# Attention by token chunks over all heads, with TensorE's order written out by hand, half chunks paired across batches, and float32 loads cast on the chip

## The chip, the cores and the metric

The kernel runs on one core of a Trainium2 chip. The metric is the device time of one execution in microseconds (us). A core has TensorE (PE in the profile, with its weight loads as PEld), VectorE (DVE), ScalarE (ACT), GpSimd (POOL), a sync engine (SP) and 16 DMA engines.

## The reference

Eight batches, eight heads, 576 tokens, head width 64: a retention attention, and on its output a mixer with a low-rank token part and an MLP of width 2048. All inputs and the output are float32.

```python
# q, k, v: (8, 8, 576, 64)
scores = q @ k.T / sqrt(64)
gamma  = 1 - 2.0 ** (-5 - arange(8))                 # one per head
Dmat   = where(i >= j, gamma ** (i - j), 0)
x      = ((scores * Dmat) @ v)                       # heads joined: (8, 576, 512)
h      = x.transpose(0, 2, 1) @ U @ V                # U (576, 32), V (32, 576)
u      = x + h.transpose(0, 2, 1)
out    = u + relu(u @ w_ch1) @ w_ch2                 # (512, 2048), (2048, 512)
```

The decay splits into a factor of the query's position and one of the key's, so that a chunk of tokens needs its own masked scores and one 64 by 64 state per head (the sum of k transposed times v over the chunks before it).

## The kernel before

576 tokens are four chunks of 128 and one of 64 (`NC` = 5). All matmuls are in bfloat16.

`qkv_load(b)` loads a batch on POOL's DMA queue, one load for each of q, k, v and each chunk (L141); the load casts float32 to bfloat16 on its way. It clears the half chunk's other 64 rows (L138), and POOL multiplies v by `vscale`, the key factor (L150).

`attention_hp` treats one pair of heads over all five chunks. It transposes q (L164) and k (L174); the copies out of PSUM are DVE's with the query factor `qsrow` (L167) and ACT's (L177). The state products of four chunks (L185) are summed by DVE in pieces of 64 rows (L195, L200). Scores are matmuls of 64 rows, eight into `blk_sc` (L219) and two for the last chunk, `blk_sct` (L238), masked by DVE (L227, L244). Then come the matmuls with v (L256), the copy to `x_t` (L264, L265), the matmuls of 64 rows with the state (L271), and DVE adds these to `x_t` (L280, L286). PSUM pool `ps_sc` has two buffers, `ps_out` one tile of two banks.

`mixer_head(b)` forms `ps_at` from U and x (L301), copies it (L308), makes `ps_h` for each chunk with V (L312), adds x (L318), transposes u (L325) and copies to `uT_t` (L330).

`mlp_tail(b)` computes W1 in 16 blocks of the width and two halves of 288 tokens, four matmuls each (L341) with the Relu behind (L347), then W2 for each of five chunks, 16 matmuls of 512 columns (L356); the fifth has 64 rows, which takes as many columns. DVE adds u (L363), SP stores (L367).

The main program loads batches 0 and 1 and the weights, does the attention of batch 0, and then for each b: loads b+2, `mixer_head(b)` at high priority, `attention(b+1)`, `mlp_tail(b)`. A planner sets the order of every engine's instructions: it takes what its own timing has ready, earlier program text first, and puts in the semaphores. So attention matmuls fill in among MLP matmuls.

Of the kernel before, what the change touches and what calls it, by code (L numbers as in the profile page):

```python
# [12 lines left out]
ALU = mybir.AluOpType  # L13


@with_exitstack
def kernel(
# [18 lines left out]
    NC = (S + P - 1) // P  # L36
    LAST = S - (NC - 1) * P
    SP = NC * P
# [3 lines left out]
    MAIN = (NC - 1) * P  # L42
    HTOK = 288

    gammas = [1.0 - 2.0 ** (-5.0 - h) for h in range(H)]
    scale = 1.0 / math.sqrt(D)

    consts = ctx.enter_context(tc.tile_pool(name="consts", bufs=1))
    qkv_pool = ctx.enter_context(tc.tile_pool(name="qkv_pool", bufs=3))
    attT_pool = ctx.enter_context(tc.tile_pool(name="attT_pool", bufs=2))  # L50
    ret_pool = ctx.enter_context(tc.tile_pool(name="ret_pool", bufs=4))
    ssb_pool = ctx.enter_context(tc.tile_pool(name="ssb_pool", bufs=8))
    xu_pool = ctx.enter_context(tc.tile_pool(name="xu_pool", bufs=2))
    mix_pool = ctx.enter_context(tc.tile_pool(name="mix_pool", bufs=2))
    y1_pool = ctx.enter_context(tc.tile_pool(name="y1_pool", bufs=2))
    osb_pool = ctx.enter_context(tc.tile_pool(name="osb_pool", bufs=4))

    ps_sc = ctx.enter_context(tc.tile_pool(name="ps_sc", bufs=2, space=bass.MemoryType.PSUM))
    ps_out = ctx.enter_context(tc.tile_pool(name="ps_out", bufs=1, space=bass.MemoryType.PSUM))
    ps_mix = ctx.enter_context(tc.tile_pool(name="ps_mix", bufs=1, space=bass.MemoryType.PSUM))  # L60
    ps_big = ctx.enter_context(tc.tile_pool(name="ps_big", bufs=3, space=bass.MemoryType.PSUM))

    ident = consts.tile([P, P], BF16)
    make_identity(nc, ident)

    maskbin = consts.tile([P, P], BF16)
    make_upper_triangular(nc, maskbin, val=1.0, diag=True)

    iota_col = consts.tile([P, SP], FP32)
    iota_pc = consts.tile([P, NC], FP32)  # L70
    lnbias = consts.tile([P, 1], FP32)
    qsrow = consts.tile([P, NHP, SP], BF16)
    vscale = consts.tile([P, H, NC], FP32)
    U_sb = consts.tile([P, NC, P], BF16)
    V_sb = consts.tile([P, SP], BF16)

    def make_early_consts():
        nc.gpsimd.iota(
            iota_pc, pattern=[[P, NC]], base=0, channel_multiplier=1,
            allow_small_or_imprecise_dtypes=True,  # L80
        )
        nc.gpsimd.memset(lnbias, math.log(scale))
        for h in range(H):
            g = gammas[h]
            nc.scalar.activation(
                out=vscale[:, h, :],
                in_=iota_pc,
                func=AF.Exp,
                bias=lnbias,
                scale=-math.log(g),  # L90
            )

    def make_consts():
        nc.gpsimd.iota(
            iota_col, pattern=[[1, SP]], base=0, channel_multiplier=0,
            allow_small_or_imprecise_dtypes=True,
        )

        for hp in range(NHP):
            for hl in range(2):  # L100
                g = gammas[2 * hp + hl]
                nc.scalar.activation(
                    out=qsrow[hl * 64:(hl + 1) * 64, hp, :],
                    in_=iota_col[hl * 64:(hl + 1) * 64, :],
                    func=AF.Exp,
                    bias=0.0,
                    scale=math.log(g),
                )

        nc.gpsimd.memset(U_sb, 0.0)  # L110
        nc.gpsimd.dma_start(
            out=U_sb[:, 0:NC - 1, 0:R],
            in_=moe_U[0:MAIN, :].rearrange("(c p) r -> p c r", p=P),
        )
        nc.gpsimd.dma_start(out=U_sb[0:LAST, NC - 1, 0:R], in_=moe_U[MAIN:S, :])

        nc.gpsimd.memset(V_sb, 0.0)
        nc.gpsimd.dma_start(out=V_sb[0:R, 0:S], in_=moe_V)

    w1_sb = consts.tile([P, NCC, dff], BF16)  # L120
    w2_sb = consts.tile([P, NF, dm], BF16)

    def load_weights():
        for cc in range(NCC):
            nc.gpsimd.dma_start(
                out=w1_sb[:, cc, :], in_=moe_w_ch1[cc * P:(cc + 1) * P, :]
            )
        for fc in range(NF):
            nc.gpsimd.dma_start(
                out=w2_sb[:, fc, :], in_=moe_w_ch2[fc * P:(fc + 1) * P, :]  # L130
            )

    def qkv_load(b):
        q_all = qkv_pool.tile([P, NC, H, 64], BF16, tag="q_all", name="q_all")
        k_all = qkv_pool.tile([P, NC, H, 64], BF16, tag="k_all", name="k_all")
        v_all = qkv_pool.tile([P, NC, H, 64], BF16, tag="v_all", name="v_all")
        for t_dram, t_sb in ((q, q_all), (k, k_all), (v, v_all)):
            nc.gpsimd.memset(t_sb[LAST:P, NC - 1, :, :], 0.0)  # L138
            for c in range(NC):
                L = P if c < NC - 1 else LAST  # L140
                nc.gpsimd.dma_start(  # L141
                    out=t_sb[0:L, c, :, :],
                    in_=t_dram[b, :, c * P:c * P + L, :].rearrange(
                        "h s d -> s h d"
                    ),
                )
        vs = vscale.rearrange("p h c -> p c h")
        vs_b = vs[:, :, :, None].to_broadcast([P, NC, H, 64])
        for c in range(NC):
            nc.gpsimd.tensor_tensor(  # L150
                out=v_all[:, c, :, :],
                in0=v_all[:, c, :, :],
                in1=vs_b[:, c, :, :],
                op=ALU.mult,
            )
        return q_all, k_all, v_all

    def attention_hp(hp, q_all, k_all, v_all, x_t):
        h0 = 2 * hp

        psq = ps_sc.tile([P, NC, P], BF16, tag="ps_sc", name="psq")
        for c in range(NC):
            q2d = q_all[:, c, h0:h0 + 2, :].rearrange("p h d -> p (h d)")
            nc.tensor.transpose(psq[:, c, :], q2d, ident)  # L164
        qT = attT_pool.tile([P, SP], BF16, tag="qT", name="qT")
        psq_flat = psq.rearrange("p c i -> p (c i)")
        nc.vector.tensor_tensor(  # L167
            out=qT, in0=psq_flat, in1=qsrow[:, hp, :], op=ALU.mult
        )

        psk = ps_sc.tile([P, NC, P], BF16, tag="ps_sc", name="psk")
        for c in range(NC):
            k2d = k_all[:, c, h0:h0 + 2, :].rearrange("p h d -> p (h d)")
            nc.tensor.transpose(psk[:, c, :], k2d, ident)  # L174
        kT = attT_pool.tile([P, SP], BF16, tag="kT", name="kT")
        psk_flat = psk.rearrange("p c i -> p (c i)")
        nc.any.tensor_copy(out=kT, in_=psk_flat)  # L177

        po = ps_out.tile([P, 8, P], FP32, tag="ps_out", name="po")

        S_list = []
        for c in range(NC - 1):
            k2d = k_all[:, c, h0:h0 + 2, :].rearrange("p h d -> p (h d)")
            v2d = v_all[:, c, h0:h0 + 2, :].rearrange("p h d -> p (h d)")
            nc.tensor.matmul(  # L185
                po[:, 5 + (c % 2), :],
                k2d,
                v2d,
                start=True, stop=True,
            )  # L190
            S_cur = ssb_pool.tile([P, 64], BF16, tag="S_sb", name="S_cur")
            for hl in range(2):
                pb = hl * 64
                if c == 0:
                    nc.vector.tensor_copy(  # L195
                        out=S_cur[pb:pb + 64, :],
                        in_=po[pb:pb + 64, 5 + (c % 2), pb:pb + 64],
                    )
                else:
                    nc.vector.tensor_tensor(  # L200
                        out=S_cur[pb:pb + 64, :],
                        in0=po[pb:pb + 64, 5 + (c % 2), pb:pb + 64],
                        in1=S_list[c - 1][pb:pb + 64, :],
                        op=ALU.add,
                    )
            S_list.append(S_cur)

        ret_map = {}
        sc_h = []
        rt_h = []  # L210
        for hl in range(2):
            blk_sc = ps_sc.tile([P, 4, P], FP32, tag="ps_sc", name="blk_sc")
            ret_m = ret_pool.tile([P, 4, P], BF16, tag="retT", name="ret_m")
            sc_h.append(blk_sc)
            rt_h.append(ret_m)
        for c in range(NC - 1):
            for hl in range(2):
                pb = hl * 64
                nc.tensor.matmul(  # L219
                    sc_h[hl][:, c, :],  # L220
                    kT[pb:pb + 64, c * P:(c + 1) * P],
# [161 lines left out]
    for b in range(B):  # L383
        if b + 2 < B:
            qkv_tiles[b + 2] = qkv_load(b + 2)
# [41 lines left out]
```

## Time and profile before

| | |
|---|---|
| median of 3 runs | 432.22 us (432.12 to 432.56) |
| the profiled execution, first to last instruction (span) | 429.9 us |
| busy: PE / PEld / DVE / ACT / POOL | 391.8 / 232.2 / 220.7 / 171.9 / 169.2 us |
| first MLP matmul (W1 of batch 0) | 60.34 us |
| one period of the steady part (b = 2) | 182.64 to 230.01 us |
| last MLP, alone | from 392.77 us |
| DMA packets | 121,333, of them 116,048 on POOL's queue |

The profile comes from one execution, of which the page gives the span and no other time; the runs of the table lie 2.2 to 2.7 us above that span. Times in the page are us unless marked ns. A busy share is an average over stages; matmuls are pipelined, and a duration of one includes the time until its result has left the array, so the spacing of starts, not the durations, tells what a matmul costs in a dense stretch.

### The profile page before, as it was taken

The numbers are of one execution on the slowest core, as the hardware profiler recorded it, in microseconds if no ns is written. First come the engines' busy times: TensorE is split into PE (matmuls) and PEld (weight loads), VectorE is DVE, ScalarE is ACT, GpSimd is POOL, SyncE is SP. The second block draws the span as 40 slices with busy tenths as digits, with TensorE's granted clock in tenths as the row PEclk, the third lists the DMA queues.
The fourth block names the chain that finished last, engine by engine and source line by source line (L and its number), as shares of the span: only waits on it lengthen the run. The fifth ranks groups of instructions, "written<-read, shape, count | busy, mean of one in ns | idle before, by whom it ended". The sixth has DMA issues, their size and how long they took to land.

```text
span 429.9 us, 8035 instructions
## 1 busy us (share of the span) xinstructions
PE 391.8 (91%) x3248; PEld 232.2 (54%) x3248; DVE 220.7 (51%) x662; ACT 171.9 (40%) x379; POOL 169.2 (39%) x220
## 2 busy tenths in 40 slices
PE   1256489999999999999999999999999999999996
PEld 0034256754675457644665467645765467546842
DVE  0166458751775448652875268643875277541011
ACT  2152136630564226630664136531663046423800
POOL 9999669899986700691048500000000000000000
PEclk9999999999999999999999999999999999999999
DMA  9999899899969910891079810011000100011011
GB/s 71 93 65 109 157 202 156 51 140 117 163 39 87 109 61 2 58 135 73 14 48 81 113 38 2 2 49 63 2 1 26 66 21 2 2 50 61 2 49 62
DMA packets 121333, 28.38 MB, mean 66 GB/s; under 512 B 114096, under 2 KB 116176, under 8 KB 121296
## 3 DMA queue, kind: packets, MB, share of 16 engines
q0 software_dynamic: 116048, 18.43, 58.1%
q1 hardware_dynamic: 5248, 9.44, 6.3%
q8 instruction: 25, 0.41, 0.4%
q14 instruction: 12, 0.10, 0.1%
HBM read 36.85 MB, written 9.44 MB: 108 GB/s over the span
## 4 chain that ended last, share of the span: by engine, by line
PE 87%; POOL 5%; DVE 4%; ACT 3%; issue 1%; DVEq 0%; ACTq 0%; POOLq 0%
PE po L185 3%; PE po L256 3%; PE ps_h L312 3%; PE blk_sc L219 3%; PE ps_at L301 2%; PE psq L164 2%; PE psk L174 2%; PE ps_ut L325 2%; PE po L271 2%; PE blk_sct L238 2%; ACT x_t L264 1%; POOL q_all L141 1%; POOL k_all L141 1%; POOL v_all L150 1%; POOL v_all L141 1%
## 5 line engine op out<-in xcount | busy, mean ns | idle before, releaser
L341 PEld LDWEIGHTS <-w_sb 128*128 128x128 bf16 x1024 | 88.6, 98 | 27.7 <-issue 1.4
L356 PEld LDWEIGHTS <-y_t 128*128 128x128 bf16 (+1 forms) x640 | 61.5, 100 | 65.3 <-issue 3.4
L177 ACT COPY kT<-psk 128x640 bf16<-128x640 bf16 x32 | 22.2, 693 | 96.0 <-PE psk L174 96.0
L200 DVE TENSOR_TENSOR S_cur<-po,S_cur 64x64 bf16<-64x64 f32 x192 | 42.1, 219 | 20.0 <-PE po L185 16.4
L227 DVE TENSOR_TENSOR ret_m<-blk_sc,maskbin 128x512 bf16<-128x512 f32 x64 | 42.5, 687 | 12.7 <-PE blk_sc L219 8.3
L150 POOL TENSOR_TENSOR v_all<-v_all,vscale 128x512 bf16<-128x512 bf16 x40 | 41.4, 1053 | 5.1 <-DMA v_all<-in_v_dram 4.6
L318 DVE TENSOR_TENSOR u_t<-ps_h,x_t 128x512 bf16<-128x512 f32 x40 | 27.6, 690 | 27.3 <-PE ps_h L312 27.3
L185 PE MATMUL po<-v_all,k_all 128*128 128x128 bf16 x128 | 29.2, 228 | 9.3 <-POOL v_all L150 4.3
L330 ACT COPY uT_t<-ps_ut 128x512 bf16<-128x512 bf16 x40 | 23.4, 586 | 33.8 <-PE ps_ut L325 33.8
L141 POOL DMA_DIRECT2D q_all<-in_q_dram x40 | 34.2, 877 | 0.0
L141 POOL DMA_DIRECT2D v_all<-in_v_dram x40 | 34.0, 920 | 0.0
L141 POOL DMA_DIRECT2D k_all<-in_k_dram x40 | 33.7, 876 | 0.0
L280 DVE TENSOR_TENSOR x_t<-po,x_t 128x192 bf16<-128x192 f32 x64 | 22.5, 352 | 7.8 <-PE po L271 5.5
L195 DVE CAST S_cur<-po 64x64 bf16<-64x64 f32 x64 | 14.0, 219 | 24.0 <-PE po L185 23.0
L264 ACT CAST x_t<-po 128x512 bf16<-128x512 f32 x31 | 18.2, 586 | 17.7 <-PE po L256 16.9
L164 PE MATMUL psq<-ident,q_all 128*128 128x128 bf16 x160 | 16.6, 232 | 8.6 <-DMA q_all<-in_q_dram 8.5
L138 POOL MEMSET q_all<- 64x512 bf16 x8 | 4.2, 519 | 49.7 <-PE psq L164 49.5
L185 PEld LDWEIGHTS <-k_all 128*128 128x128 bf16 x128 | 12.7, 100 | 18.1 <-issue 4.4
L325 PEld LDWEIGHTS <-u_t 128*128 128x128 bf16 x160 | 12.5, 102 | 14.4 <-issue 7.2
L219 PE MATMUL blk_sc<-qT,kT 64*128 64x128 bf16 x256 | 15.7, 229 | 4.7 <-DVE qT L167 2.5
L174 PE MATMUL psk<-ident,k_all 128*128 128x128 bf16 x160 | 16.0, 230 | 3.9 <-DMA k_all<-in_k_dram 3.7
L167 DVE TENSOR_TENSOR qT<-psq,qsrow 128x640 bf16<-128x640 bf16 x32 | 15.6, 488 | 7.0 <-PE psq L164 5.1
(637 smaller groups left out, 717.4 us busy)
## 6 DMA issues: line engine op xcount, KB each, us to landing
out_dram<-o_sb SPq DMA_DIRECT2D x32, 256.0 KB, 2.0
q_all<-in_q_dram POOLq DMA_DIRECT2D x32, 128.0 KB, 4.4
k_all<-in_k_dram POOLq DMA_DIRECT2D x32, 128.0 KB, 4.3
v_all<-in_v_dram POOLq DMA_DIRECT2D x32, 128.0 KB, 4.6
w_sb<-in_moe_w_ch_dram POOLq DMA_DIRECT2D x4, 512.0 KB, 7.8
w_sb<-in_moe_w_ch_dram POOLq DMA_DIRECT2D x16, 128.0 KB, 5.8
out_dram<-o_sb SPq DMA_DIRECT2D x8, 128.0 KB, 2.2
q_all<-in_q_dram POOLq DMA_DIRECT2D x8, 64.0 KB, 4.7
```

Source lines behind the costliest of these rows:

```text
L141: nc.gpsimd.dma_start(out=t_sb[0:L, c, :, :], in_=t_dram[b, :, c * P:c * P + L, :].rearrange("h s d -> s h d"),)
L150: nc.gpsimd.tensor_tensor(out=v_all[:, c, :, :], in0=v_all[:, c, :, :], in1=vs_b[:, c, :, :], op=ALU.mult,)
L164: nc.tensor.transpose(psq[:, c, :], q2d, ident)
L174: nc.tensor.transpose(psk[:, c, :], k2d, ident)
L185: nc.tensor.matmul(po[:, 5 + (c % 2), :], k2d, v2d, start=True, stop=True,)
L200: nc.vector.tensor_tensor(out=S_cur[pb:pb + 64, :], in0=po[pb:pb + 64, 5 + (c % 2), pb:pb + 64], in1=S_list[c - 1][pb:pb + 64, :], op=ALU.add,
L219: nc.tensor.matmul(sc_h[hl][:, c, :], kT[pb:pb + 64, c * P:(c + 1) * P], qT[pb:pb + 64, c * P:(c + 1) * P], start=True, stop=True,)
L227: nc.vector.tensor_tensor(out=rt_h[hl][:, :, :], in0=sc_h[hl][:, :, :], in1=maskbin[:, None, :].to_broadcast([P, 4, P]), op=ALU.mult,)
L318: nc.vector.tensor_tensor(out=u_t[:, c, :], in0=ps_h, in1=x_t[:, c, :], op=ALU.add)
L330: nc.any.tensor_copy(out=uT_t[:, :, c * P:(c + 1) * P], in_=ps_ut[:, 0:NCC, :])
L341: nc.tensor.matmul(ps_y1[:, 0:HTOK], w1_sb[:, cc, f * P:(f + 1) * P], uT_t[:, cc, t0:t0 + HTOK], start=(cc == 0), stop=(cc == NCC - 1),)
L356: nc.tensor.matmul(ps_y2[0:L, :], y1_t[:, f, tcn * P:tcn * P + L], w2_sb[:, f, :], start=(f == 0), stop=(f == NF - 1),)
```

## The change

Nearly the whole body is rewritten.

- Loads: q, k, v of one chunk go as float32 on SP's queue into one `stage` tile (four buffers); DVE casts q and k to bfloat16 in one copy, POOL casts v and multiplies it by `vscale`.
- Attention is done by chunk, over all eight heads at a time: `T` transposes q and k (8 transposes, one copy by ACT), `ST` adds the state products of four head pairs into one PSUM bank across chunks and copies them with a block-diagonal mask, `SC` makes the scores of eight heads in two banks and masks them in one DVE operation, `RV` multiplies with v and adds the state's share in the same PSUM bank (128-row matmuls, since the state is block-diagonal). The query factor moves to the copy of x, one DVE operation per chunk.
- The half chunks of an even and the following odd batch share tiles: the even batch uses rows 0 to 63 of `x_half` and `u_half`, the odd batch rows 64 to 127. The MLP of an even batch has four chunks, of an odd batch five (the shared one first). W1 works on 512 tokens, or twice 320; W2 on full chunks only.
- PSUM: `ps_t`, `ps_s`, `ps_o` one bank each, `ps_sc` one tile of two banks, `ps_big` three.
- TensorE's order is written out: `interleave` merges two lists, the MLP of batch b and the attention and mixer of batch b+1, so that both advance by the same share of their given costs. The other engines' orders are still planned.
- Consts: the eight `qsrow` exponentials go; `qscale` and `vscale` are one exponential each over (chunk, head). DVE clears the shared tiles, U and V. W1 is loaded in 16 pieces (four width blocks by four), W2 in eight.

```diff
+def interleave(main, fill):
+    tm = sum(c for c, _ in main) or 1
+    tf = sum(c for c, _ in fill) or 1
...
+        if j >= len(fill) or (i < len(main) and dm / tm <= df / tf):
+            dm += main[i][0]; main[i][1](); i += 1
+        else:
+            df += fill[j][0]; fill[j][1](); j += 1
...
+    stage = ctx.enter_context(tc.tile_pool(name="stage", bufs=4))
+    qkv_pool = ctx.enter_context(tc.tile_pool(name="qkv_pool", bufs=9))
+    osb_pool = ctx.enter_context(tc.tile_pool(name="osb_pool", bufs=3))
...
+    def load_chunk(b, c):
+        t = qkvh[b % 2] if is_half(b, c) else qkv_pool.tile([P, 3, H, D], BF16, ...)
+        f = stage.tile([P, 3, H, D], FP32, tag="stage", name="stage_t")
+        for j, dram in ((1, k), (0, q), (2, v)):
+            nc.sync.dma_start(
+                out=f[rows, j, :, :],
+                in_=dram[b, :, t0:t0 + L, :].rearrange("h s d -> s h d"),
+            )
+        nc.vector.tensor_copy(out=t[rows, 0:2, :, :], in_=f[rows, 0:2, :, :])
+        nc.gpsimd.tensor_tensor(
+            out=t[rows, 2, :, :], in0=f[rows, 2, :, :],
+            in1=vscale[rows, c, :, None].to_broadcast([L, H, D]), op=ALU.mult,
+        )
...
+        def T(c):        # ps_t: 8 transposes of 128 columns
+            nc.scalar.activation(out=qkT, in_=pst, func=AF.Copy)
+        def ST(c):       # ps_s: 4 matmuls of 128 columns, kept over the chunks
+            nc.vector.tensor_tensor(out=s_sb, in0=pss, in1=bdm[...], op=ALU.mult)
+        def SC(c):       # ps_sc: 8 matmuls of 64 rows, 128 columns (64 in a half chunk)
+            nc.vector.tensor_tensor(out=rv[:, :, :, cols], in0=psc[:, :, :, 0:n],
+                                    in1=tri[...], op=ALU.mult)
+        def RV(c):       # ps_o: 8 matmuls of 64 columns, 4 of 128 with the state
+            nc.vector.tensor_tensor(out=xt[rows, :], in0=po[rows, :],
+                                    in1=qscale[rows, c, :, None]..., op=ALU.mult)
...
+        for s in range(NC + 2):
+            if s < NC:
+                add(T, s, 460)
+            if 0 <= s - 2:
+                add(RV, s - 2, 450)
+            if s < NC - 1:
+                add(ST, s, 220)
+            if 0 <= s - 1 < NC:
+                add(SC, s - 1, 450)
...
+    def mixer_items(b, x_tiles, u_tiles, pair):
+        # MA(c): ps_s += U[c] x[c], 512 columns, ACT copies after the last
+        # MH(c): V[c] a, 512 columns, ps_o or ps_s in turn; DVE adds x
+        # MT(c): ps_t, 4 transposes of u; ACT copies to uT
+        for c in range(NC):
+            items.append((220, lambda c=c: MA(c)))
+        for c in range(NC + 1):
+            if c < NC:
+                items.append((220, lambda c=c: MH(c)))
+            if c >= 1 and not (par == 0 and c - 1 == NC - 1):
+                items.append((230, lambda c=c - 1: MT(c)))
...
+    def mlp_items(b, u_tiles, pair):
+        nch = 4 if par == 0 else 5
+        segs = [(0, 512)] if par == 0 else [(0, 320), (320, 320)]
+        # Y1(f, t0, n): 4 matmuls of n columns, ACT Relu; Y2(c, f0): 4 of 512 columns,
+        # after 16 of them DVE adds u and SP stores
+        for f in range(NF):
+            for t0, n in segs:
+                items.append((n * 4 / 2.4, lambda f=f, t0=t0, n=n: Y1(f, t0, n)))
+        for c in range(nch):
+            for f0 in range(0, NF, 4):
+                items.append((853, lambda c=c, f0=f0: Y2(c, f0)))
...
+    early_consts()
+    zero_halves()
+    load_batch(0)
+    late_consts()
+    load_w1()
+    load_batch(1)
+    load_w2()
+    with tc.manual_schedule(engines={PE}):
+        interleave([], front_items(0))
+        for b in range(B):
+            if b + 2 < B:
+                load_batch(b + 2)
+            fill = front_items(b + 1) if b + 1 < B else []
+            interleave(mlp_items(b, us[b], pairs[b // 2]), fill)
```

In what follows a name with a number, such as RV3, is that step for chunk 3, and front(b) is the list of attention and mixer steps of batch b.

More of the change, by code (lines that the diff above doesn't have):

```diff
@@ new lines @@
+    ps_t = ctx.enter_context(tc.tile_pool(name="ps_t", bufs=1, space=bass.MemoryType.PSUM))
+    ps_sc = ctx.enter_context(tc.tile_pool(name="ps_sc", bufs=1, space=bass.MemoryType.PSUM))
+    ps_s = ctx.enter_context(tc.tile_pool(name="ps_s", bufs=1, space=bass.MemoryType.PSUM))
+    ps_o = ctx.enter_context(tc.tile_pool(name="ps_o", bufs=1, space=bass.MemoryType.PSUM))
+    ps_big = ctx.enter_context(tc.tile_pool(name="ps_big", bufs=3, space=bass.MemoryType.PSUM))
+    ident = consts.tile([P, P], BF16, name="ident")
@@ L120 @@
[L120 to L153, printed above, removed]
@@ L154, in qkv_load @@
                 op=ALU.mult,
             )
[L156 to L184, printed above, removed]
-            nc.tensor.matmul(
-                po[:, 5 + (c % 2), :],
-                k2d,
-                v2d,
@@ L189, in attention_hp @@
                 start=True, stop=True,
             )
[L191 to L221, printed above, removed]
-                    qT[pb:pb + 64, c * P:(c + 1) * P],
-                    start=True, stop=True,
-                )
-                ret_map[(c, hl)] = (rt_h[hl], c)
@@ L293, in attention @@
[L293 to L323 removed]
+                out=ut[rows, :], in0=ph[rows, :], in1=x_tiles[c][rows, :], op=ALU.add
+            )
```

475 lines of the change are left out of this document (272 added, 203 removed).

## The prediction

> **What bounds the kernel now.** I read the page's engine totals and slices first, then the chain of waits in order of time for stage marks, then the busy times by stage, then the timeline of TensorE.
>
> ```profile
> span 429.9 us, 8035 instructions
> PE 391.8 (91%) x3248; PEld 232.2 (54%) x3248; DVE 220.7 (51%) x662; ACT 171.9 (40%) x379; POOL 169.2 (39%) x220
> PE   1256489999999999999999999999999999999996
> PEclk9999999999999999999999999999999999999999
> PE 87%; POOL 5%; DVE 4%; ACT 3%; issue 1%; DVEq 0%; ACTq 0%; POOLq 0%
> ...
> 0.00:60.34 60.34, 26.74 (x199) 14.75 (x200) 24.47 (x82) 16.61 (x32) 52.05 (x79) 1.00 1.23 110
> 182.64:230.01 47.37, 47.33 (x407) 28.08 (x408) 27.59 (x83) 20.24 (x45) 19.19 (x25) 1.00 0.66 63
> 392.77:429.90 37.13, 33.18 (x209) 20.33 (x208) 4.13 (x6) 13.16 (x32) 0.00 (x0) 1.00 0.11 36
> ...
> 60.34 0.97 PE ps_y_925 L341 x4
> 182.64 1.19 PE ps_y_2499 L356 x5
> 230.01 1.19 PE ps_y_3190 L356 x5
> 392.77 0.60 PE ps_y_5393 L341 x4
> 408.56 3.45 PE ps_y_5585 L356 x16
> ```
>
> The window rows give length, then busy time of PE, PEld, DVE, ACT, POOL. Three stages are to be seen. The head lasts until the first MLP matmul at 60.34, with PE busy for 26.74 of it. Then periods of 47.37, each one batch's MLP with the next batch's attention and mixer inside it, PE busy 47.33: TensorE bounds them. Last, one MLP alone from 392.77; its W1 half takes 408.56-392.77 = 15.79 (128 matmuls of 288 columns, 0.1234 each), a W2 chunk 3.45 (16 of 512 columns, 0.2156 each). MLP matmuls thus take 15.79 + 5 x 3.45 = 33.0; with the slightly longer last chunk I use 33.2, so attention and mixer cost 47.37-33.2 = 14.2 a period. Check: 60.34 + 8 x 33.2 + 7 x 14.2 + 3.9 (37.13-33.2, the last add and store) = 429.2, against a span of 429.9. The median of the runs, 432.22, lies 2.3 above the span; I add that at the end.
>
> **MLP.** Pairing removes the padded half chunk: W2 goes from 10 chunks a pair of batches to 9. W1 keeps its columns, as 64 matmuls of 512 (even batch) and 128 of 320 (odd). A 320-column matmul, on the line between 288 and 512 columns, is 0.1366. Even MLP: 64 x 0.2156 + 4 x 3.45 = 27.6; odd: 128 x 0.1366 + 5 x 3.45 = 34.7. Four of each: 249.2, where 265.6 stands now: -16.4, plain column counting on the bounding engine.
>
> **Attention and mixer on TensorE.** Spacing comes from starts in the steady timeline:
>
> ```profile
> 183.66 1.03 PE L301 MATMUL ps_at<-x_t,U_sb 128*128 128x512 bf16 x4
> ...
> 203.21 0.45 PE L164 MATMUL psq<-ident,q_all 128*128 128x128 bf16 x5
> 203.50 0.44 PE L174 MATMUL psk<-ident,k_all 128*128 128x128 bf16 x5
> ...
> 206.52 0.23 PE L238 MATMUL blk_sct<-qT,kT 64*128 64x128 bf16 x1
> 206.68 0.42 PE L341 MATMUL ps_y_3016<-uT_t,w_sb 128*128 128x288 bf16 x2
> ...
> 208.11 0.40 PE L256 MATMUL po<-v_all,ret_m 128*128 128x64 bf16 x8
> 208.34 0.19 PE L256 MATMUL po<-v_all,ret_tl 128*128 128x64 bf16 x1
> ...
> 210.00 0.40 PE L219 MATMUL blk_sc<-qT,kT 64*128 64x128 bf16 x8
> 210.33 0.30 PE L341 MATMUL ps_y_3034<-uT_t,w_sb 128*128 128x288 bf16 x1
> ```
>
> 128 columns: 0.29/5 = 0.057 each. 64 columns: 0.23/8 = 0.029. 64-row scores: 0.33/8 = 0.041. A lone 64-row matmul holds the engine 206.68-206.52 = 0.16 instead of 0.057, so going to 64 rows and back costs about 0.1 beside an idle gap ahead of it. Before, per batch: 76 + 8 matmuls of 128 columns 4.8, 32 scores 1.3, 40 of 64 columns 1.2, 32 small ones of 64 rows at some 0.02, 0.6, ten of 512 columns 2.2: 10.1. The other 14.2-10.1 = 4.1 belong to 14 runs of 64-row matmuls in a period, 0.29 a run, switches and waits together. After: 40 transposes, 16 state products, 16 state uses (now 128 rows with a block-diagonal state) and 18 transposes of u: 90 x 0.057 = 5.1; scores 32 x 0.041 + 8 x 0.03 = 1.6; 40 x 0.029 = 1.2; ten of 512 2.2: 10.1. But 64-row runs are only the five score blocks: 5 x 0.29 = 1.5. So 11.6 a batch, seven times 81.2 in place of 99.4.
>
> **New hand-offs.** TensorE's order is now fixed, and ps_t, ps_sc, ps_s, ps_o have one buffer. Prices:
>
> ```profile
> L227 DVE TENSOR_TENSOR ret_m<-blk_sc,maskbin 128x512 bf16<-128x512 f32 x64 | 42.5, 687 | 12.7 <-PE blk_sc L219 8.3 <-PE po L256 3.8
> L244 DVE TENSOR_TENSOR ret_tl<-blk_sct,maskbin 128x128 bf16<-128x128 f32 x64 | 16.3, 283 | 1.0 <-PE blk_sct L238 0.6
> L318 DVE TENSOR_TENSOR u_t<-ps_h,x_t 128x512 bf16<-128x512 f32 x40 | 27.6, 690 | 27.3 <-PE ps_h L312 27.3
> L330 ACT COPY uT_t<-ps_ut 128x512 bf16<-128x512 bf16 x40 | 23.4, 586 | 33.8 <-PE ps_ut L325 33.8
> L177 ACT COPY kT<-psk 128x640 bf16<-128x640 bf16 x32 | 22.2, 693 | 96.0 <-PE psk L174 96.0
> L265 DVE CAST x_t<-po 128x128 bf16<-128x128 f32 x7 | 2.0, 292 | 0.1
> ```
>
> DVE takes (687-283)/384 = 1.05 ns an element, so the 1,024-element score multiply takes 0.687 + 0.54 = 1.23; ACT 0.84 ns, so the 1,024-element copy of qT and kT takes 1.01. About 0.3 is lost between the last matmul's issue and the next user (0.19 of pipe end, two semaphores; my estimate from the 0.22 that a 57 ns matmul shows). Counting out the order that the diff's progress shares give: in an even MLP, RV3 and RV4 each stand one 0.86 item behind their scores: 1.53-0.86 = 0.67 each; T1 comes 1.09 after T0 and needs 1.31 plus ACT's Relu: 0.35; the last transposes of u and the next W1: 0.35; MT2: 0.13. Sum 2.2. In an odd MLP: 0.67, 0.13 and, since the next even W1 reads all four chunks of uT, 0.586 + 0.3 = 0.9: 1.7. Over four even and three odd periods: 13.9. The rest of the waits has two items of cover. Cover is thin where DVE is late; its sum per batch is five casts, four state masks at 0.69, four full scores at 1.23 and a half at 0.69, five x at 0.69, five u at 0.69, 4.5 outputs at 0.69: 18.4 plus casts. A cast of 1,024 float32 from SBUF stands in no row; by the PSUM cast's 292 at 128 elements and 1.05 ns it is 1.23, at two elements a tick about 0.7, so 3.5 to 6.2 in all. I take 6.2, nearest row. DVE 24.6 of 44, ACT 17 to 21 (16 copies of 0.59, or 32 of 0.43; 5 x 1.01; 5 x 0.59): neither bounds.
>
> **Head.** The present one is a string of POOL issues, loads and table work:
>
> ```profile
> 2.34 4.39 POOL L141 DMA_DIRECT2D q_all<-in_q_dram  x5
> 7.14 4.24 POOL L141 DMA_DIRECT2D k_all<-in_k_dram  x5
> 10.92 0.29 PE L174 MATMUL psk<-ident,k_all 128*128 128x128 bf16 x1 [0.94 <-DMA k_all<-in_k_dram]
> 14.40 0.29 PE L174 MATMUL psk<-ident,k_all 128*128 128x128 bf16 x1 [1.03 <-DMA k_all<-in_k_dram]
> 20.83 5.98 ACT L102 ACTIVATE qsrow<-iota_col 64x640 bf16<-64x640 f32 x8 [4.99 <-POOL iota_col L94]
> 31.71 0.69 PE L164 MATMUL psq<-ident,q_all 128*128 128x128 bf16 x5
> 32.19 0.74 PE L174 MATMUL psk<-ident,k_all 128*128 128x128 bf16 x5
> 51.06 1.86 PE L301 MATMUL ps_at<-x_t,U_sb 128*128 128x512 bf16 x4 [0.92 <-DVE x_t L280]
> q0 software_dynamic: 116048, 18.43, 58.1%
> L150 POOL TENSOR_TENSOR v_all<-v_all,vscale 128x512 bf16<-128x512 bf16 x40 | 41.4, 1053 | 5.1 <-DMA v_all<-in_v_dram 4.6
> L138 POOL MEMSET q_all<- 64x512 bf16 x8 | 4.2, 519 | 49.7 <-PE psq L164 49.5
> ```
>
> The 120 loads leave POOL for SP, which now only stores; POOL's issues there (0.86 each) and qsrow's 5.98 go. POOL keeps v's scaling at 1.05 a chunk, five small loads, 16 of W1 instead of 4 and 8 of W2 instead of 16, W1 behind batch 0's scaling; all that ends before 43. A load of the new kind (1,024 packets of 256 bytes, no cast) isn't in the trace: loads of as many packets land (14.40-10.92)/3 = 1.16 apart now, and packet time (58.1% x 16 x 429.9 / 116,048 = 34 ns, over 16 engines) allows at most 2.2 a load. I take 1.2 (same packet count) and keep 2.2. Chunk 0 lands at 6 to 8. DVE first clears some 9,000 elements a partition (519/512, about 1 ns each): ready at 10. Then it is the head's limit: batch 0's casts, masks, scores and x are 6.2 + 2.75 + 5.6 + 3.4 = 18, batch 1's casts, ahead in program order, 6, waits some 2; then the mixer's serial end, 7 (a copy, five 0.69 adds with matmuls between, a copy). First MLP matmul at 10 + 18 + 6 + 2 + 7 = 43. Bounds: 34 (casts at 0.7, none of batch 1) and 47 (2.2 a load: last chunk at 33, 7 of attention behind it, 7 of mixer).
>
> PEclk reads 9 throughout, yet five transposes take 32.19-31.71 = 0.48 in the head against 0.29, and the four ps_at matmuls 1.86 against 1.03: the sparse head runs at about half rate whatever that column says, and the 7 above has it. The Trainium skill, TensorE: Matmul & The Clock Gate, Part 1, has the rule: half clock until some 3.4 us of sustained work. By it, and the cadence agrees, front(0) without MLP stays slow, while waits under 1 us later don't; by the clock column the head would be some 2 shorter, 391.
>
> **Sum.** 43 + 249.2 + 81.2 + 13.9 + 3.9 = 391.2 of span, + 2.3 = 393.5; I say 393.
>
> **Rivals.** *Clean interleaving:* the waits vanish in TensorE's queue and the head, its ten casts at 0.7, is 37: 393.5-13.9-6 = 373. For it: PE idles 0.04 in 47.37 now. Against: the planner there could reorder, a fixed order can't. 22%.
>
> *DVE stands at the fifth chunk:* stage has four tiles, so chunk 4's loads wait for chunk 0's cast and scaling; if the casts stand together in DVE's queue, it waits three loads plus 2.7 of latency less three casts of 1.23: 5.6 at 2.2 a load, 2.3 for a half chunk, 2.5 and 0.7 at 1.2. What the wait holds: masks, scores, x, and so TensorE. Stores behind loads on SP, with three o_sb, act alike. Six batches: 10 to 24, 403 to 417. For: DVE has no such load waits now. Against: the order of DVE is planned, not program order. 20%.
>
> *Slower:* every cast stands in DVE's queue until its chunk lands, none covered by earlier loads: 24.6 + 13.5 loads a batch x 2.2 = 54.3 a period against TensorE's 44.8; 6 x 9.5 gives 450. It costs more than no change (432) from 6.5 a period on, which is 2.0 a load. Against: four tiles of staging run ahead. 10%.
>
> *A shared port:* if DVE's casts and POOL's scaling exclude each other, each of five casts in the head may wait 1.05: head 48, 399; in a period DVE has 29.9 of 44, nothing. The Trainium skill, SBUF — State Buffer, Who interferes with whom, says that a cast in a two-port mode and GpSimd block each other wholly. No row here shows it, since DVE reads PSUM now. 8%.
>
> **Numbers.** Forecast 38% with 382 to 400; clean 22% (368 to 382); port 8% (395 to 402); fifth chunk 20% (400 to 422); slower 10%; 2% between. 369 to 422 leaves out some 14%. Faster by over 0.2% (what a measurement of this kernel tells from none) 0.87, within 0.02, slower 0.11.
>
> **What would show it.** The first W1 matmul near 43; W2 chunks of 3.45, 36 of them; a period of some 41 (even MLP) and 48 (odd) with PE idle of about 2; idle before RV3, RV4, T1 and the first W1, released by DVE or ACT. Wrong if DVE idles on the stage tiles' loads, if loads take over 2 each, or if five score blocks don't cut the 4.1.

## The result, and the profile after

| | before | after |
|---|---|---|
| median, us | 432.17 (432.02 to 432.56, 4 runs) | 396.17 (395.43 to 396.57, 4 runs) |
| ratio to before | | 0.9166, 95% interval 0.9153 to 0.9179 |
| span of the profiled execution, us | 429.9 | 394.6 |
| first MLP matmul, us | 60.34 | 52.84 |
| seven periods, us | 332.43 | 302.72 |
| last MLP to the end, us | 37.13 | 39.04 |

The change saves 36.0 us; 393 had been forecast, with a range of 369 to 422. Of the 35.3 us by which the span is shorter, 7.5 lie in the head, 29.7 in the periods, and the end gives 1.9 back. The page of the kernel after, cut to the lines that answer to those shown of before:

```profile
span 394.6 us, 6659 instructions
...
PE 348.4 (88%) x2784; PEld 200.0 (51%) x2784; DVE 183.1 (46%) x249; ACT 156.2 (40%) x279; POOL 64.2 (16%) x83
...
PE   1244489999999999899999999899999999999996
...
PEclk9999959999999999999999999999999999999999
DMA  8999999726995599485149500011001100010012
...
q1 hardware_dynamic: 117696, 37.76, 43.4%
q0 software_dynamic: 5744, 4.31, 7.2%
```

TensorE is still the bound, with the first five slices (49 us) as the weak place. The DMA row beneath stands at 8 and 9 in the same slices: the engines that move data are full while TensorE is not. The loads of q, k and v have left POOL's software queue (q0) for SP's (q1); those of the weights stay on POOL's.

The same execution cut at the first W1 matmul of each MLP; the columns are the stretch, its length, the busy time (and instructions) of PE, PEld, DVE, ACT and POOL, granted clock, DMA share and GB/s:

```profile
0.00:52.84 52.84, 20.18 (x178) 13.58 (x179) 24.80 (x48) 9.84 (x13) 27.40 (x49) 0.95 1.12 194
52.84:94.67 41.83, 40.86 (x310) 21.41 (x310) 22.37 (x31) 16.91 (x26) 8.99 (x9) 0.94 0.69 148
94.67:141.32 46.65, 45.47 (x390) 27.94 (x388) 24.82 (x34) 21.46 (x43) 10.67 (x10) 1.00 0.87 180
141.32:181.94 40.62, 38.67 (x311) 20.29 (x310) 24.07 (x29) 16.84 (x26) 7.29 (x7) 1.00 0.90 182
181.94:228.58 46.64, 45.46 (x389) 27.96 (x387) 25.20 (x30) 21.46 (x43) 5.21 (x5) 1.00 0.47 109
228.58:269.21 40.63, 38.67 (x311) 20.31 (x311) 21.24 (x27) 16.84 (x26) 4.68 (x4) 1.00 0.07 27
269.21:315.85 46.64, 45.46 (x389) 27.96 (x387) 19.29 (x25) 21.45 (x43) 0.00 (x0) 1.00 0.08 30
315.85:355.56 39.71, 38.67 (x311) 20.30 (x311) 17.20 (x23) 16.84 (x26) 0.00 (x0) 1.00 0.07 27
355.56:394.60 39.04, 34.97 (x211) 20.24 (x208) 4.13 (x6) 14.54 (x33) 0.00 (x0) 1.00 0.11 41
```

Periods of one kind are alike: in the steady part those with the MLP of an even batch take 40.6, those of an odd one 46.6. In the head the engines leave much time free: TensorE is busy 20.18 of 52.84 us and DVE 24.80, while 194 GB/s are moved. The head of the wait list of TensorE in the kernel after (total us, times, longest):

```profile
PE pst L207 <- DVE qkv L184: 14.7, 4, 6.2
PE po L270 <- DVE ret L257: 8.2, 12, 1.4
PE pss L225 <- POOL qkv L185: 6.7, 4, 2.6
PE pu L351 <- DVE ut L344: 3.8, 2, 3.2
```

Taken for the head alone, the list has the first, third and fourth line in full: transposes, state products and the transposes of u wait there for what DVE and POOL make of the loads. Of the second, the use of the scores by `RV`, 1.4 is the head's and the rest is the hand-off that the prediction priced. What the head waits for stands on DVE and POOL, here single rows of their timelines (start, duration, in brackets the idle time before it and what ended it), with two of TensorE's:

```profile
14.24 0.69 DVE L184 CAST qkv<-stage_t 128x1024 bf16<-128x1024 f32 x1 [7.78 <-DMA stage_t<-in_q_dram]
33.94 1.06 POOL L185 TENSOR_TENSOR qkvh_122<-stage_t,vscale 64x512 bf16<-64x512 f32 x1
41.28 0.68 DVE L287 TENSOR_TENSOR x_half<-po,qscale 64x512 bf16<-64x512 f32 x1 [1.20 <-POOL qkvh_123 L185]
47.66 0.69 DVE L184 CAST qkv<-stage_t 128x1024 bf16<-128x1024 f32 x1 [2.56 <-DMA stage_t<-in_q_dram]
49.01 0.61 PE L351 MATMUL pu<-ident,ut 128*128 128x128 bf16 x4 [3.24 <-DVE ut L344]
52.84 1.87 PE L390 MATMUL ps_y_553<-uT_474,w_sb 128*128 128x512 bf16 x4 [0.69 <-ACT uT_474 L354]
```

DVE stands 7.78 us for chunk 1, batch 0's last v is scaled at 33.94, its attention ends at 41.96. Then, in the mixer, DVE stands 2.56 us at a cast for batch 1, and the add of u, which is next in its queue, waits with it: TensorE idles 3.24. DVE's own wait list has these two and no other wait of a cast for a load:

```profile
DVE qkv L184 <- DMA stage_t<-in_q_dram: 10.3, 2, 7.8
```

### The profile page after: what moved, and what is told of

It is laid out like the page before. It is cut to its first block, busy times and chain, and to the rows that moved or that the text cites. A ratio compares the mean times of both kernels' runs of the same rounds, so it can differ in the third digit from the quotient of the medians.

```text
span 394.6 us, 6659 instructions
## 1 busy us (share of the span) xinstructions
PE 348.4 (88%) x2784; PEld 200.0 (51%) x2784; DVE 183.1 (46%) x249; ACT 156.2 (40%) x279; POOL 64.2 (16%) x83
## 5 line engine op out<-in xcount | busy, mean ns | idle before, releaser
L390 PEld LDWEIGHTS <-w_sb 128*128 128x128 bf16 x768 | 70.4, 98 | 39.1 <-issue 4.7
L185 POOL TENSOR_TENSOR qkv<-stage_t,vscale 128x512 bf16<-128x512 f32 x32 | 34.7, 1085 | 128.3 <-DMA stage_t<-in_v_dram 65.3
L257 DVE TENSOR_TENSOR ret<-psc,tri 128x1024 bf16<-128x1024 f32 x32 | 39.1, 1221 | 9.3 <-PE psc L246 9.1
L184 DVE CAST qkv<-stage_t 128x1024 bf16<-128x1024 f32 x32 | 30.9, 966 | 24.2 <-PE po L270 12.1
L232 DVE TENSOR_TENSOR s_sb<-pss,bdm 128x512 bf16<-128x512 f32 x32 | 22.1, 689 | 41.5 <-PE pss L225 41.5
L216 ACT ACTIVATE qkT<-pst 128x1024 bf16<-128x1024 bf16 x32 | 32.8, 1024 | 20.1 <-PE pst L207 19.1
L287 DVE TENSOR_TENSOR xt<-po,qscale 128x512 bf16<-128x512 f32 x32 | 22.0, 688 | 33.3 <-PE po L277 25.0
L207 PE MATMUL pst<-ident,qkv 128*128 128x128 bf16 x256 | 21.3, 231 | 15.4 <-DVE qkv L184 14.7
L207 PEld LDWEIGHTS <-qkv 128*128 128x128 bf16 x256 | 18.1, 104 | 22.1 <-DVE qkv L184 15.5
L344 DVE TENSOR_TENSOR ut<-ph,xt 128x512 bf16<-128x512 f32 x32 | 22.0, 690 | 11.9 <-PE ph L335 11.7
L270 PEld LDWEIGHTS <-ret 128*128 128x128 bf16 x256 | 11.6, 102 | 16.9 <-DVE ret L257 13.8
L225 PE MATMUL pss<-qkv 128*128 128x128 bf16 x112 | 11.6, 231 | 6.7 <-POOL qkv L185 6.7
L225 PEld LDWEIGHTS <-qkv 128*128 128x128 bf16 x112 | 9.2, 103 | 11.1 <-issue 6.8
```

Of the source, the lines that this page charges most:

```text
L184: nc.vector.tensor_copy(out=t[rows, 0:2, :, :], in_=f[rows, 0:2, :, :])
L185: nc.gpsimd.tensor_tensor(out=t[rows, 2, :, :], in0=f[rows, 2, :, :], in1=vscale[rows, c, :, None].to_broadcast([L, H, D]), op=ALU.mult,)
L207: nc.tensor.transpose(pst[:, j * NHP + hp, :], t[:, j, 2 * hp:2 * hp + 2, :].rearrange("p h d -> p (h d)"), ident,)
L216: nc.scalar.activation(out=qkT, in_=pst, func=AF.Copy)
L232: nc.vector.tensor_tensor(out=s_sb, in0=pss, in1=bdm[:, None, :].to_broadcast([P, NHP, P]), op=ALU.mult,)
L257: nc.vector.tensor_tensor(out=rv[:, :, :, cols], in0=psc[:, :, :, 0:n], in1=tri[:, None, None, cols].to_broadcast([P, 2, NHP, n]), op=ALU. ...
```

## The experiments

Two questions: what holds the head, and whether the period's terms are what the prediction took them for. The times of first W1 and the periods are those of each kernel's profiled execution; after has 52.84, then 41.83, 46.65, 40.62.

**Batch 0's scaling of v on DVE** (e1): is the head late since POOL's queue puts weight loads ahead of the scaling, or since the data come late?

```diff
-        nc.gpsimd.tensor_tensor(
+        (nc.vector if b == 0 else nc.gpsimd).tensor_tensor(
             out=t[rows, 2, :, :], in0=f[rows, 2, :, :],
```

> Batch 0's v is scaled on DVE instead of POOL; all else as changed. The head (first W1 matmul at 52.84 us, 43 forecast) is the question. Theory A, POOL's queue: batch 0's scalings stand behind weight loads that POOL issues; taken off it, the state products no longer wait for POOL (6.7 us of waits), the first W1 matmul comes at 44 to 46, the time falls from 396.2 to about 388. Theory B, transfers: weights and batch 0 share the DMA engines; with nothing between them POOL issues all 24 weight loads even earlier, so batch 0 lands later, first W1 matmul at 50 to 56, time 394 to 400. Theory C, DVE's own work limits the head as the prediction had it: 3.4 us more on DVE, head 3 later, 399.

Measured: 397.96 (395.99 to 400.12), ratio 0.9211 [0.9174, 0.9248]; first W1 at 56.42. The wait moved to the other engine, as TensorE's wait list shows:

```profile
PE pss L225 <- DVE qkv L185: 10.5, 1, 10.5
```

The scaling is no earlier, but that does not clear POOL's queue, for e1 only puts another queue in its place. On DVE the first scaling stands behind the cast of chunk 1, which waits for its load, and runs at 17.05; POOL had done it at 8.71. Rows of e1's DVE:

```profile
16.10 0.69 DVE L184 CAST qkv<-stage_t 128x1024 bf16<-128x1024 f32 x1 [9.66 <-DMA stage_t<-in_q_dram]
17.05 1.23 DVE L185 TENSOR_TENSOR qkv<-stage_t,vscale 128x512 bf16<-128x512 f32 x2
```

And in after, POOL's order does cost something. Chunk 3's v was issued at 17.14 and landed 5.3 later, at 22.4; it is scaled at 28.60, behind loads of W2 that POOL issues first, and TensorE waits for it:

```profile
27.14 1.44 POOL L156 DMA_DIRECT2D w_sb<-in_moe_w_ch_dram  x2 [0.48 <-DMA w_sb<-in_moe_w_ch_dram]
28.60 1.06 POOL L185 TENSOR_TENSOR qkv<-stage_t,vscale 128x512 bf16<-128x512 f32 x1
29.71 0.58 PE L225 MATMUL pss<-qkv 128*128 128x128 bf16 x4 [1.86 <-POOL qkv L185]
```

TensorE's wait of 1.85 for chunk 2 has the same form. So e1 leaves the question open.

**W1 and W2 behind batch 0's loads** (e2): each piece's first column is first written by a small POOL copy that reads batch 0's last scaled v, so that the planner cannot issue a weight load earlier.

```diff
+    def hold_weights():
+        one = qkv[0][NC - 1][:, 2, 0, 0:1]
+        nc.gpsimd.tensor_copy(out=<first column of each W1 piece>, in_=<one, broadcast>)
+        nc.gpsimd.tensor_copy(out=<first column of each W2 piece>, in_=<one, broadcast>)
...
     late_consts()
+    hold_weights()
     load_w1()
```

> Every load of W1 and W2 waits until POOL has scaled batch 0's last chunk (a small POOL copy into each weight piece comes first and is overwritten by the load). It takes away both the queue order on POOL and the sharing of the DMA engines. A alone: as e1, first W1 matmul at 44 to 46, 388. B: batch 0's loads land alone, 13.5 loads at 1.2 us, by 20; first W1 matmul at 36 to 42, time 380 to 386, and better than e1 by over 6. C: no change, 396.

Measured: 392.40 (391.06 to 393.95), ratio 0.9093 [0.9072, 0.9115]. First W1 at 41.71, and a first period of 47.58. Rows of the timelines of this kernel, in the order of POOL, DVE and TensorE:

```profile
20.72 1.04 POOL L196 TENSOR_TENSOR qkvh<-stage_t,vscale 64x512 bf16<-64x512 f32 x1 [1.52 <-DMA stage_t<-in_v_dram]
...
8.80 1.06 DVE L195 CAST qkv<-stage_t 128x1024 bf16<-128x1024 f32 x1 [2.35 <-DMA stage_t<-in_q_dram]
33.02 0.68 DVE L298 TENSOR_TENSOR x_half<-po,qscale 64x512 bf16<-64x512 f32 x1 [1.20 <-PE po L288]
54.11 0.69 DVE L195 CAST qkv<-stage_t 128x1024 bf16<-128x1024 f32 x1 [5.90 <-DMA stage_t<-in_q_dram]
...
41.71 1.87 PE L401 MATMUL ps_y<-uT,w_sb 128*128 128x512 bf16 x4 [0.69 <-ACT uT L365]
55.46 0.61 PE L281 MATMUL po<-qkvh,reth 128*128 128x64 bf16 x8 [4.61 <-DVE reth L268]
```

Chunk 1 is cast at 8.80 instead of 14.24, the last v is scaled at 20.72 instead of 33.94, the attention ends at 33.70 instead of 41.96, and the mixer takes 8.0 instead of 10.9. So the head's 11.1 us come from the weights' loads. By which way is settled only in part, since e2 changes both the transfers and POOL's order. Chunk 1's cast waits for its load in both kernels and comes 5.4 earlier: that is the transfers' doing. TensorE's waits of 1.85 and 1.86 for scalings of landed chunks are gone: up to 3.7 is POOL's order. In the mixer no cast waits for a load any more, where after has 2.56 of DVE and with it 3.24 of TensorE. Half of the gain is paid back: the weights now come among batch 1's loads, DVE stands 5.90 us at a cast, and the score mask behind it in its queue, for which TensorE waits 4.61, is late.

**The weights in turn** (e6): W1 behind batch 0, W2 behind batch 1's third chunk.

```diff
+    def hold_w1():     # as above, for W1 alone
+        one = qkv[0][NC - 1][:, 2, 0, 0:1]
...
+    def hold_w2():     # for W2 alone
+        one = qkv[1][2][:, 2, 0, 0:1]
...
     late_consts()
+    hold_w1()
     load_w1()
     load_batch(1)
+    hold_w2()
     load_w2()
```

> Loads take turns by need: W1 waits until POOL has scaled batch 0's last chunk, W2 until it has scaled batch 1's third. Bandwidth theory: head 41.7 as in e2, and the first period loses less than the 5.8 that e2 gave back (47.58 against 41.83), since batch 1 no longer shares with W2 until its third chunk: period 42 to 45, time 385 to 389. If the first period is held by the order of DVE's queue rather than by the transfers: as e2, 392.

Measured: 390.36 (389.63 to 391.93), ratio 0.9039 [0.9012, 0.9066]; first W1 at 42.79, first period 46.10. Time and period miss what was expected, by a little over 1 us: one wait for the masked scores of 3.1 us is left, at 67.18, after DVE has stood 7.6 at a cast until 64.10. It is the eleventh cast, so that of batch 2's first chunk, which this period does not need.

**One W2 chunk too many** (e3): every even batch computes its last W2 chunk a second time and adds u, and does not store it. It prices the freed chunk.

```diff
...
-        for c in range(nch):
+        for c in list(range(nch)) + ([5 + nch] if par == 0 else []):
             for f0 in range(0, NF, 4):
```

> Each even batch computes its last W2 chunk a second time (16 matmuls and DVE's add; the second result is not stored): the padding that pairing removed, put back. If TensorE's columns count in full, as the sum had it, 4 x 3.45 = 13.8 more: 410. If the periods hold slack for it (waits of other engines, 1 to 2 us of idle a period), 4 to 8 less than that: 402 to 406.

Measured: 404.51 (404.17 to 406.70), ratio 0.9372 [0.9346, 0.9398], so 8.3 over after, not four times 3.45. The even periods grow by 1.75 (43.57, then 42.37), the last by 2.66. TensorE's wait list for `RV` shows where most of the rest is:

```profile
PE po L270 <- DVE ret L257: 3.9, 8, 1.4
```

8.2 us in after, 3.9 here: the extra items stand between scores and their use, and cover the mask. The even period from 143.03 has TensorE idle for 0.43, where after's, from 141.32, has 1.95. Of the 13.8 us of columns that pairing takes off TensorE, only some 8 come off the time in this order; the others turn into hand-off waits.

**Scores in two runs** (e4): `SC` is issued as two items of four heads, so that each batch has five more runs of 64-row matmuls. It prices a run.

```diff
...
-                add(SC, s - 1, 450)
+                add(lambda c: SC(c, 0), s - 1, 225)
+                add(lambda c: SC(c, 1), s - 1, 225)
```

> The eight score matmuls of a chunk go in two runs of four, an item apart; mask and everything else stay. Forty more runs of 64-row matmuls. At the prediction's 0.29 a run (switch and waits): 40 x 0.29 = 11.6 more, 408. At 0.1 a run, the gaps beside the score blocks in the new trace: 4 more, 400. If changing the row count costs nothing: 396.

Measured: 404.62 (404.15 to 405.39), ratio 0.9366 [0.9352, 0.9380]. Odd periods 48.35 (1.70 more), even 41.19 (0.57 more). Of the 1.70, 0.8 are a new wait for the masked half scores; the remaining 0.9 over five runs is 0.18 a run, and the even period's 0.57 gives 0.11. A run costs 0.11 to 0.18, not 0.29. The rows of after agree: W1 starts at 100.66, eight scores at 101.30, W1 again at 101.63; four W1 matmuls of 320 columns take 0.54 and eight scores 0.33, which leaves 0.10.

**Later use** (e5): `RV` stands after the next chunk's scores, the `MA` of three chunks before the last `RV`, and the last W2 item is kept until the fill list is done. No work is changed.

```diff
-            if 0 <= s - 2:
-                add(RV, s - 2, 450)
             if s < NC - 1:
                 add(ST, s, 220)
             if 0 <= s - 1 < NC:
                 add(SC, s - 1, 450)
+            if 0 <= s - 2:
+                add(RV, s - 2, 450)
...
-        return attention_items(...) + mixer_items(...)
+        return att[:-1] + mix[:3] + att[-1:] + mix[3:]
...
-        if j >= len(fill) or (i < len(main) and dm / tm <= df / tf):
+        if j >= len(fill) or (i < len(main) - 1 and dm / tm <= df / tf):
```

> Only TensorE's written order changes: RV of a chunk comes after the next chunk's SC, three MA steps come between SC4 and the last RV, and the last W2 item of an MLP is kept for after the last transposes of u. If the hand-offs named in the prediction (RV3, RV4, the first W1 after uT) are real waits, the idle of PE in the seven periods (9.4 us by the windows of the new trace) falls to 2 to 4: time 396.2 to 389 to 391, periods 39.5 and 46. If they are only apparent, since the late result returns as a later wait, 395 to 397. Head unchanged near 53.

Measured: 384.46 (383.54 to 385.49), ratio 0.8899 [0.8878, 0.8921], 11.7 us below after: more than was expected. Of the 11.1 that the span is shorter, 8.5 lie in the periods and 2.4 in the head, which had been expected to stay. A steady even and odd period of this kernel:

```profile
136.73:176.29 39.56, 38.64 (x311) 20.59 (x310) 23.62 (x29) 17.44 (x27) 7.28 (x7) 1.00 0.91 184
176.29:221.26 44.97, 44.97 (x388) 28.08 (x387) 24.37 (x29) 20.90 (x42) 5.21 (x5) 1.00 0.56 125
```

In the odd period TensorE is busy 44.97 of 44.97, where after has 45.46 of 46.64; in the even one it is idle for 0.92, where after has 1.95. Over the seven periods its idle time falls from 9.5 to 3.1, as had been expected. The hand-offs were real time, and TensorE's order made them.

**Both orders, then the casts off DVE** (e7 is e5 with e6; e10 is e7 with the casts of batches 1 to 7 on POOL). If DVE's standing at casts is what the first period still loses, taking the casts out of its queue ends the loss, though the data come no sooner.

```diff
-        nc.vector.tensor_copy(out=t[rows, 0:2, :, :], in_=f[rows, 0:2, :, :])
+        (nc.vector if b == 0 else nc.gpsimd).tensor_copy(out=t[rows, 0:2, :, :], in_=f[rows, 0:2, :, :])
```

> e5 and e6 together. If head and hand-offs are separate terms, the gains add: 396.2 less e5's (5 to 7) less e6's (7 to 11): 378 to 384. If they share a cause (DVE), less than the sum.

> e7 with the casts of batches 1 to 7 on POOL instead of DVE (batch 0's stay on DVE). Theory queue: in the first period DVE stands at a cast whose chunk hasn't landed and holds masks and x behind it; then period 0 falls from e7's 48.07 to 42 to 44 and the time from 379.8 to 374 to 376. Theory transfers: front(1) needs the same late chunks whoever casts them; period 0 stays at 46 to 48, time 378 to 381. If POOL, slower a cast, is late in the steady periods: those grow over 39.3 and 45.0, time over 381.

Measured: e7 379.81 (379.41 to 382.85), ratio 0.8806 [0.8772, 0.8841], first W1 38.09 and first period 48.07; e10 372.96 (372.07 to 373.48), ratio 0.8638 [0.8624, 0.8653], 37.39 and 41.48. In e7, the rows of DVE and then of TensorE:

```profile
63.36 0.69 DVE L198 CAST qkv<-stage_t 128x1024 bf16<-128x1024 f32 x1 [8.91 <-DMA stage_t<-in_q_dram]
64.57 0.68 DVE L301 TENSOR_TENSOR xt<-po,qscale 128x512 bf16<-128x512 f32 x1
...
65.31 0.61 PE L284 MATMUL po<-qkv,ret 128*128 128x64 bf16 x8 [5.50 <-DVE xt L301]
```

DVE stands 8.91 us at a cast whose chunk is under way, again the eleventh, for batch 2; the copy to `xt` behind it, whose operand was ready, is late, its PSUM bank stays taken, and TensorE waits 5.50. In e10 this wait is gone and the first period is 6.6 shorter, like a steady one within 2.3. The eleventh cast runs at 63.94 there, on POOL, so the data come no sooner; only what stood behind it is freed. POOL has room for the casts: it is busy 24.66 of the first period's 41.48. The casts' row of e10:

```profile
L198 POOL CAST qkv<-stage_t 128x1024 bf16<-128x1024 f32 x28 | 29.1, 1038 | 80.6 <-PE po L284 47.7
```

**A busy TensorE in the head** (e9 on e6, e11 on e10): eight matmuls of 128 columns on the identity, into a bank that nobody reads, behind each step of batch 0's attention and mixer. If the half rate in the head costs time, this buys it.

```diff
...
+        for cost, fn in front_items(0):
+            head += [(cost, fn), (1, warm)]
-        interleave([], front_items(0))
+        interleave([], head)
```

> e6 with eight more 128-column matmuls (identity, result unused) after each TensorE step of batch 0's attention and mixer: they add 0.45 to 0.86 a step in which TensorE would mostly wait, and keep it at work. If the half rate of the head costs about 2 (the prediction's price) plus the first 4 us of MLP at half rate (2 more): 3 to 4 less than e6. If the added work delays the head more than the clock gives: equal or 1 to 5 more.

> e10 with e9's eight idle matmuls after each step of front(0). In e9 the warm TensorE had reached the mixer 2.3 us earlier than in e6, and then DVE stood 3.6 at batch 1's cast. With that cast off DVE the gain of the full clock should stay: first W1 matmul 2 to 3 earlier than in e10 and its first 4 us at full rate, time 2 to 4 below e10. If the transfers hold the head or period 0: equal to e10.

Measured: e9 396.46 (395.35 to 397.32), ratio 0.9175 [0.9155, 0.9195], 6.1 worse than e6: first W1 45.34, first period 49.80. e11 372.76 (372.15 to 373.36), ratio 0.8630 [0.8617, 0.8643], equal to e10. In e9 the rate rose, as these rows of its TensorE show, and fell again at one wait for DVE, which stood at a cast:

```profile
35.72 0.38 PE L349 MATMUL ph<-a_sb,Vbig 128*128 128x512 bf16 x1
35.93 0.61 PE L470 MATMUL ps_warm<-ident 128*128 128x128 bf16 x8
40.11 0.61 PE L365 MATMUL pu<-ident,ut 128*128 128x128 bf16 x4 [3.56 <-DVE ut L358]
40.51 1.06 PE L470 MATMUL ps_warm<-ident 128*128 128x128 bf16 x8
41.36 0.63 PE L349 MATMUL ph<-a_sb,Vbig 128*128 128x512 bf16 x1
```

In e9's first period TensorE then waits 8.12 for masked scores, until 66.80 (3.06 in e6), behind DVE's eleventh cast, which runs at 64.19 (64.10 in e6): the chunk comes at the same time however early TensorE is.

In e11 the first W1 runs at full rate (four matmuls in 1.02 instead of 1.87) but no sooner, at 38.05 (37.39 in e10), and the idle matmuls take TensorE's time too: it is busy for 28.80 of the head, in e10 for 18.76. W2 starts at 58.49 instead of 59.12, and then TensorE's wait list has transfers in it:

```profile
PE ps_y L415 <- DMA w_sb<-in_moe_w_ch_dram: 1.5, 2, 1.1
```

A faster TensorE arrives sooner at weights that have not come. e10 and e11 are the fastest versions, 23 us below after.

## Why the prediction was right, and where not

The terms against the profiled execution of after (us):

| term | forecast | measured | difference |
|---|---|---|---|
| head, to the first W1 | 43 | 52.84 | +9.8 |
| four even periods | 4 x 41.4 | 162.79 | -2.8 |
| three odd periods | 3 x 48.0 | 139.93 | -4.1 |
| last MLP and end | 38.6 | 39.04 | +0.4 |
| time outside the span | 2.3 | 1.8 | -0.5 |

The median lies 3.2 over the 393. That it is no more is luck: an error of 10 in the head met one of 7 the other way in the periods. One of the prediction's own signs of being wrong came true, that DVE idles on the stage tiles' loads, but only in the head.

- **The head is the mis-sized term.** The step that failed is "W1 behind batch 0's scaling; all that ends before 43": the prediction counted the weights' loads as issues on POOL and put their transfers at nothing. POOL issues W1 from 1.82 on, before any scaling. The head of after moves 194 GB/s on the mean, weights among it, and batch 0's 15 loads have landed by 30.1, 1.9 apart on the mean; in e2, without the weights, by 20.7, 1.2 apart, which is the price that the prediction took. The Trainium skill, DMA: Bandwidth & Descriptors, Issuing engines are not separate DMA queues, says that transfers run on the same 16 engines and interleave whichever engine started them; e2's chunk 1, cast 5.4 earlier, agrees. Up to 3.7 more is POOL's order, weight loads issued ahead of scalings; no run takes away one of the two alone.
- **The bound of 47** had this course in part: last chunk at 33 (33.94 measured), 7 of attention behind it (8.0). The mixer after that took 10.9 instead of 7, of which 3.24 is the wait behind a cast for batch 1.
- **The 43 itself was met for partly wrong reasons.** e2's head is 41.71 without the weights. Yet DVE is not its limit, as the prediction had it: it started casting at 5.44, not 10 (the clears, priced by a row of POOL, ran as 32-bit words: 0.48 for 1,024 elements a partition); a cast takes 0.68, and up to 1.53 beside POOL, not 1.23 each; and DVE idles 1.1 to 2.0 us ahead of each copy of x while TensorE and ACT take turns. Smaller work and longer waits balanced.
- **MLP columns** held: 34.7 + 3.9 forecast from the last MLP on, 39.04 measured; its W1 half took 17.69, where 128 x 0.1366 is 17.5.
- **Attention and mixer, 11.6 a batch:** e5's odd period with no idle time, 44.97, leaves 10.3 beside 34.7. Its even period of 39.24 (the one from 221.26) has TensorE busy for 38.49, which leaves 10.9 beside 27.6. The price of a 64-row run was too high (0.11 to 0.18 instead of 0.29), which is 0.6 to 0.9 a batch and covers the even one's 0.7; the remainder of the odd one's 1.3 is not settled.
- **Hand-offs, 13.9 in all:** the mechanism is shown by e5, which brings TensorE's idle time in the periods from 9.5 to 3.1 by its order alone; the size was too large. After's 9.5 are 1.95 in a steady even one (2.2 forecast; 0.97 and 1.04 in the first and the last), 1.18 in an odd one (1.7 forecast). By the wait list the even period from 141.32 has 1.9 for `RV` (1.3 forecast). The odd one before it has 0.4 for `RV` (0.67) and 0.7 for the first W1 of the next MLP (0.9). T1, `MT2` and the first W1 after an even MLP, which the prediction also priced, have no line there.
- **Clean interleaving** (373) did not happen in after. It was possible: e10 is at 372.96 with a head of 37.39, but with the fixed order rearranged, the weights held back and casts on POOL, not by a planner.
- **DVE stands at loads** (403 to 417): the mechanism is real, and took place in the head and at the mixer (7.78, 2.56), where the rival as told (the fifth chunk, six batches) had none of it: in after no cast of the seven periods waits for a load. It came back in the first period when TensorE got there sooner (e2, e6, e7, e9), and e10 shows it by taking the casts of batches 1 to 7 out of DVE's queue.
- **Slower** (450) needed loads that keep every period waiting. The transfers are without a break for 75 us only (213 GB/s from 70 to 75, 7 from 75 to 80), and the periods' casts never wait for one.
- **A shared port** (399): the delay exists (below), but in after's head no cast ran beside a scaling (they took 0.67 to 0.94), so it cost nothing there. In the periods some do, and take up to 1.58, where DVE has room: it is busy 25.20 of 46.64 at most.
- **Clock:** the head's half rate is there as forecast: four matmuls of 512 columns in the mixer take 1.70 (40.97 to 42.67), where 4 x 0.2156 is 0.86. Not priced was the first period, with TensorE busy for 40.86 against 38.67 in the later even ones, at a granted clock of 0.94. What the full rate alone would be worth no run shows: e11 has it by added matmuls, which brings the first period's busy time from 40.31 (e10) to 38.87, and the time stays the same.

## What to carry to other kernels

When loads are moved to another queue, add up the bytes of everything that is in flight in the same stretch, weights included, and order the transfers by first use; a queue with a free issuing engine is no free transfer, and loads that an engine issues hold up its own work behind them. In an engine's fixed order, an instruction that waits for a load stands in front of others that are ready: put such casts on an engine whose next instructions are not urgent (here POOL, e10). Where a bound engine's order is written by hand, leave other work between a producer and its use (e5), and count work that is saved there only as far as it was not covering such a wait.

## What the runs showed of the hardware

- A float32 to bfloat16 cast from SBUF on DVE takes 0.68 for 1,024 elements a partition, and up to 1.58 (after) when a scaling by POOL, which reads and writes SBUF too, has started just before. Whoever starts first goes on. In e2, two pairs:

```profile
18.16 1.04 POOL L196 TENSOR_TENSOR qkv<-stage_t,vscale 128x512 bf16<-128x512 f32 x1 [3.01 <-DMA stage_t<-in_v_dram]
36.89 1.44 POOL L196 TENSOR_TENSOR qkv<-stage_t,vscale 128x512 bf16<-128x512 f32 x1
...
18.21 1.53 DVE L195 CAST qkv<-stage_t 128x1024 bf16<-128x1024 f32 x1
36.75 0.68 DVE L195 CAST qkv<-stage_t 128x1024 bf16<-128x1024 f32 x1
```

  At 18.2 POOL is 0.05 ahead and the cast takes 0.85 more; at 36.8 the cast is 0.14 ahead and POOL's operation takes 0.40 more. The rule of the Trainium skill that the prediction weighed (SBUF — State Buffer, Who interferes with whom) has the loser blocked for the whole of the other's operation; the trace agrees in kind, and nearly in size: 0.99 of POOL's operation was left in the first pair, 0.54 of the cast in the second.
- TensorE's rate fell to half after a wait of 3.24 us (after: one matmul of 512 columns 0.38 at 45.39, 0.63 at 49.41) and of 3.56 (e9, the rows above), and there the granted clock shows it: its row of after has the 5 in the sixth slice, 49 to 59. Earlier it does not: a matmul of 512 columns takes 0.63 at 42.67, in a slice of 9, and the four before it start at 40.97, 0.43 each. In a sparse stretch these rows tell the rate, not that column.
- POOL casts 1,024 elements a partition in 1.04 us; in e10 it took the casts of seven of the eight batches, and the steady periods stayed at 39.23 and 44.97.
